# Scores of the first batch from float32 q and k, two heads on 64 rows each, in a fused attention and expert kernel

## The chip, the cores and the metric

The kernel runs on one core of one Trainium2 chip. The metric is the device time of one execution in microseconds (us). Three runs of the kernel before took 1341.06, 1344.57 and 1346.83 us; their median, 1344.57 us, is the time before.

## The reference: what is computed

Three layers in a row, in float32:

```python
# attention: batch 4, 8 heads, 576 tokens, head size 64; q, k, v are randn * 0.1
scores = scale * np.matmul(q, k.transpose(0, 1, 3, 2))
kth = np.partition(scores, -top_k, axis=-1)[..., -top_k:-top_k + 1]
mask = scores >= kth
scores = np.where(mask, scores, -1000000000.0)
...
return np.matmul(attn, v).astype(np.float32)
# gated layer: x is (2304, 512), w_gate and w_val (512, 1536), w_out (1536, 512)
gate = 1.0 / (1.0 + np.exp(-(x @ w_gate)))
val = x @ w_val
return (gate * val @ w_out).astype(np.float32)
# experts: 8 of (512, 1024) and (1024, 512), the two best of a token by noisy logits
h = np.maximum(x[mask] @ w1[e], 0.0)
out[mask] += top2_w[mask, k, None] * (h @ w2[e])
```

`top_k` is 32 and `scale` is 1/8. Which 32 scores of a row are kept, and which two experts a token goes to, are choices between close numbers, so products are carried to more than float16 throughout.

## The kernel before, in words

The work goes in order of the batch: for each of 4 batches, 5 tiles of queries (four of 128 rows, one of 64) and 4 pairs of heads make up the units, 20 a batch. A unit with 128 queries holds two tiles of scores, one for each head of the pair; a unit with the last 64 queries holds one tile, the two heads above each other. So a batch has 36 tiles of scores, each 128 by 576.

What happens to a tile: TensorE makes the scores into the one score buffer `ps` of two banks, 288 keys in each (line 348, or 351 for the tile of 64 queries); ScalarE copies them to `sS` (line 356); VectorE finds candidates, eight instructions a tile (line 365), and the best of them (lines 371 and 374); GpSimd scales two of these into a bias and a cut (line 391, with the constants `facs`); ScalarE takes the sign of score minus cut (line 400) and the exponential (line 383); GpSimd multiplies score and sign (line 406); VectorE ranks that (line 413) and masks the exponentials (line 428). Then TensorE transposes them (lines 457, 475, 477), ScalarE copies the transposes out, and TensorE multiplies with v in float32 (line 498), each head on 64 columns of the array. `xch` holds the result for a chunk of tokens, and once a chunk is full the gated layer runs on it (lines 538 and 577); the experts come at the end (lines 808 and 834).

Score products run in float16. Each number is split into two halves, a high one (the number times 64, rounded to float16) and a low one (what is left). For the first batch, `kq_ops` with `first` set loads k and q of a head pair twice each, so that all 64 dimensions of a head stand on rows 0 to 63 and again on rows 64 to 127 (line 216). ScalarE makes high halves (lines 220 and 221), VectorE the low ones (lines 222 and 224); q ends up with the high half above and the low half below, and k has high halves in both places in one tile and low halves in both in another. A product over 128 rows is then (q high + q low) times one half of k, and two of them, summed in the bank, make the score. Later batches get the same halves by another route (lines 235 to 252): ScalarE and GpSimd make them, and DMAs put them in place.

Weights of the gated layer come as pairs of 32-bit words and are unpacked in 36 pieces of 512 KB (`weight_piece`, line 275 on): VectorE takes the upper words apart (lines 281, 282), ScalarE the lower ones (283), GpSimd adds them (286), then halves are made (287, 289, 291, 292). Pieces are staged in the buffers `st`, three of them, which the q and k of the kernel before also use.

The order in which instructions stand on each engine is made before the program runs, by `Plan`: every operation is given with an engine, a planned duration, a priority, what it depends on and which buffers it takes and frees; `Plan.run` plays this through and issues, on each engine, the ready operation with the lowest priority number whose buffers are free. `CAPS` has the number of buffers of each kind: 3 `st`, 5 `khl`, 6 `sS`, 1 `ps`. Each engine then runs its instructions strictly in that order, and an instruction that waits holds all behind it. SP issues the loads, in order too.

## Time and profile before

| | |
|---|---|
| median of three runs | 1344.57 us |
| the profiled execution | 1342.8 us, its span 1341.0 us |
| TensorE busy (PE) | 1193.8 us, 89% |
| VectorE busy (DVE) | 872.2 us, 65% |
| ScalarE busy (ACT) | 800.6 us, 60% |
| GpSimd busy (POOL) | 743.0 us, 55% |
| score products of tiles with 128 queries (line 348), 512 records | 95.2 us |
| granted TensorE clock, mean | 0.955 |

Read it as a program of several parts, since the shares of the whole span mix them. The span begins with attention of the first batch and the unpacking of weights, goes on with attention and the gated layer beside each other, and ends with the experts. A granted clock of 1.00 stands for 2.4 GHz and 0.50 for 1.2 GHz; a value between is a mean over both.

### The profile page before, as it was taken

The numbers are of one execution on the slowest core, as the hardware profiler recorded it, in microseconds if no ns is written. First come the engines' busy times: TensorE is split into PE (matmuls) and PEld (weight loads), VectorE is DVE, ScalarE is ACT, GpSimd is POOL, SyncE is SP. The second block draws the span as 40 slices with busy tenths as digits, with TensorE's granted clock in tenths as the row PEclk, the third lists the DMA queues.
The fourth block names the chain that finished last, engine by engine and source line by source line (L and its number), as shares of the span: only waits on it lengthen the run. The fifth ranks groups of instructions, "written<-read, shape, count | busy, mean of one in ns | idle before, by whom it ended". The sixth has DMA issues, their size and how long they took to land. (4 is left out here: it accounts for less than half of the span.)

```text
span 1341.0 us, 29639 instructions
## 1 busy us (share of the span) xinstructions
PE 1193.8 (89%) x10669; PEld 878.2 (65%) x10670; DVE 872.2 (65%) x3616; ACT 800.6 (60%) x1796; POOL 743.0 (55%) x1004
## 2 busy tenths in 40 slices
PE   2456478699999999999999999989999999999997
PEld 1235356487676777786786876877666666676674
DVE  5998998888788688788888778545114234243111
ACT  4767778787777777786787776755214334243221
POOL 2789998788476776666775566342322222322221
PEclk9668689799899999999999999999999999999999
DMA  8433332344002500003300001357636576576441
GB/s 179 141 95 117 125 111 71 97 114 171 17 2 72 158 1 10 10 9 92 106 2 1 19 9 33 111 153 218 109 67 177 98 182 168 111 194 129 73 74 22
DMA packets 105616, 122.30 MB, mean 91 GB/s; under 512 B 56689, under 2 KB 66033, under 8 KB 105458
## 3 DMA queue, kind: packets, MB, share of 16 engines
q1 hardware_dynamic: 95346, 100.33, 27.5%
q0 software_dynamic: 10112, 19.97, 8.0%
q8 instruction: 86, 1.41, 0.4%
q14 instruction: 72, 0.59, 0.2%
HBM read 79.58 MB, written 20.63 MB: 75 GB/s over the span
## 5 line engine op out<-in xcount | busy, mean ns | idle before, releaser
L538 PEld LDWEIGHTS <-w 128*128 128x128 f16 x3456 | 275.3, 100 | 49.4 <-issue 21.7
L538 PE MATMUL mm<-xch,w 128*128 128x256 f16 (+1 forms) x2880 | 284.1, 254 | 17.8 <-DVE th L548 8.2
L816 DVE SCALAR_TENSOR_TENSOR g<-mm,g 128x256 f16<-128x256 f32 (+1 forms) x192 | 71.9, 379 | 242.5 <-ACT g L813 235.0
L406 POOL TENSOR_TENSOR y<-sS,sg 128x576 f32<-128x576 f32 x144 | 194.3, 1349 | 9.1
L808 PE MATMUL mm<-xch,w 128*128 128x256 f16 (+1 forms) x2016 | 190.3, 255 | 0.0
L808 PEld LDWEIGHTS <-w 128*128 128x128 f16 x2016 | 170.3, 98 | 23.4
L365 DVE MAX8 cand<-sS 128x8 f32<-128x72 f32 x1152 | 166.7, 217 | 21.6 <-ACT sS L356 21.2
L834 PEld LDWEIGHTS <-g 128*128 128x128 f16 x960 | 92.7, 98 | 105.6 <-DVE g L816 2.8
L577 PE MATMUL mm<-w,g 128*128 128x512 f16 x648 | 156.5, 385 | 4.1 <-POOL w L292 2.2
L428 DVE SCALAR_TENSOR_TENSOR e<-sS,good,e 128x576 f32<-128x576 f32 x144 | 144.7, 1026 | 2.1 <-ACT e L383 1.1
L348 PE MATMUL ps<-khl,qs 128*128 128x288 f16 x512 | 95.2, 315 | 57.0 <-ACT sS L356 39.4
L790 POOL DMA_INDIRECT v<-xd,ids x40 | 47.6, 1190 | 167.7 <-DVE ws L780 162.2
L813 ACT ACTIVATE g<-mm 128x256 f16<-128x256 f32 (+1 forms) x192 | 66.2, 347 | 118.0 <-PE mm L808 110.1
L846 POOL DMA_INDIRECT out<-e,ids x40 | 63.8, 1594 | 127.3 <-ACT e L843 58.7
L400 ACT ACTIVATE sg<-sS,m 128x576 bf16<-128x576 f32 x144 | 110.5, 769 | 35.4 <-POOL m L391 35.4
L413 DVE MAX8 good<-y 128x8 f32<-128x584 f32 x144 | 109.9, 763 | 28.6 <-POOL y L406 24.1
L555 POOL TENSOR_TENSOR g<-th,g 128x128 f16<-128x128 f32 (+1 forms) x144 | 92.5, 646 | 62.2 <-ACT g L552 59.6
L498 PE MATMUL tp<-pt,v 128*64 128x128 f32 (+3 forms) x1600 | 117.5, 285 | 5.4 <-ACT pt L464 2.6
L834 PE MATMUL tp<-w,g 128*128 128x512 f16 x504 | 115.3, 379 | 1.2 <-DVE g L816 1.2
L498 PEld LDWEIGHTS tp<-pt,v 128*64 128x64 f32 (+1 forms) x1600 | 85.0, 143 | 41.0 <-issue 23.9
L457 PE MATMUL tp<-ident,e 128*128 128x128 f32 x576 | 89.5, 292 | 24.6 <-DVE e L428 23.5
L577 PEld LDWEIGHTS <-g 128*128 128x128 f16 x648 | 63.0, 99 | 69.6 <-issue 8.5
(162 smaller groups left out, 2069.4 us busy)
## 6 DMA issues: line engine op xcount, KB each, us to landing
st<-w SPq DMA_DIRECT2D x64, 512.0 KB
khl<-st SPq DMA_DIRECT2D x48, 144.0 KB
st<-w_gate SPq DMA_DIRECT2D x12, 512.0 KB
st<-w_val SPq DMA_DIRECT2D x12, 512.0 KB
st<-w_out SPq DMA_DIRECT2D x12, 512.0 KB
st<-k_t SPq DMA_DIRECT2D x20, 288.0 KB
st<-q_t SPq DMA_DIRECT2D x20, 288.0 KB
out<-x SPq DMA_DIRECT2D x6, 768.0 KB
```

Source lines behind the costliest of these rows:

```text
L348: P.matmul(o, kqr.qs[:, t, u.q0:u.q0 + 128], kqr.khl[:, c, t, ks], start=c == 0, stop=c == 1)
L365: V.max(T[t].cand[:, 8 * c:8 * c + 8], T[t].s[:, 72 * c:72 * c + 72])
L400: A.activation(T[t].sg, T[t].s, AF.Sign, scale=-CUT[0], bias=T[t].m[:, 25:26], accum_out=T[t].m[:, 26:27])
L406: G.tensor_tensor(T[t].y[:, :S], T[t].s, T[t].sg, op=OP.mult)
L413: V.max(good[:, TILES - 1 - u.i - t:TILES + 7 - u.i - t], T[t].y)
L428: return lambda: V.scalar_tensor_tensor(T[t].e, T[t].s, good[:, TILES + 6 - u.i - t:TILES + 7 - u.i - t], T[t].e, op0=OP.is_ge, op1=OP.mul ...
L498: P.matmul(u.po[64 * s:64 * s + 64, :], VB[u.b, kb][1][:k, (2 * u.hp + s) * D:(2 * u.hp + s + 1) * D], rhs, start=kb == 0, stop=kb == NK - 1)
L538: P.matmul(r.ps[:, a, :], wt.t[:, a, c, kb, fo:fo + 128], ch.x[x][:, kb, :], start=i == 0, stop=i == 11)
L555: G.tensor_tensor(r.g[:, 1], r.th, r.g[:, 0], op=OP.subtract)
L577: P.matmul(r.ps, g[:, c, 128 * t:128 * t + 128], WO[f // 4].t[:, d, f % 4, :], start=f == 0 and i == 0, stop=f == 11 and i == 2)
L808: P.matmul(r.ps, W[kb].w[c][:, 0, f * 128:f * 128 + 128], q.x[:, 4 * x + kb, :], start=i == 0, stop=i == 11)
L834: P.matmul(r.ps, gs[f].g[:, c, 128 * t:128 * t + 128], W[4 + f // 2].w[d][:, f % 2, :], start=f == 0 and i == 0, stop=f == 7 and i == 2)
```

## The change

For the first batch, no halves are made. `kq_ops` loads k and q of a head pair once each, as float32, straight into the buffer that held the halves of k (two pictures of 576 float32 numbers fill a `khl` buffer exactly); head 0 of the pair then stands on rows 0 to 63, head 1 on rows 64 to 127. The score product of a head takes those 64 rows of q and of k, in float32, one product for each 288 keys. Since q and k are no longer scaled by 64 each, the factor in the exponential and in `facs` is 1/8 for the first batch, and `SC` has an entry for each batch. Batches 1 to 3 are as before. The planned duration of a tile's score product is 0.9 us in the first batch, 0.5 us in the others.

```diff
-SC = 1.0 / (8.0 * SQ * SQ)
+
+SC = [1.0 / 8.0] + [1.0 / (8.0 * SQ * SQ)] * (B - 1)
...
-    facs = const.tile([128, 2], FT, name="facs")
-    G.memset(facs[:, 0:1], -SC)
-    G.memset(facs[:, 1:2], CUT[1])
+    facs = const.tile([128, 2, 2], FT, name="facs")
+    G.memset(facs, CUT[1])
+    for b in range(2):
+        G.memset(facs[:, b, 0:1], -SC[b])
...
-                hs = [plan.tile("st") for _ in range(2)]
-                st = {}
-
-                def load(w, src):
-                    def f():
-                        if w == "k":
-                            tiles()
-                        st[w] = tile_of("st", [128, 2, S], FT)
-                        for h in range(2):
-                            nc.sync.dma_start(st[w][64 * h:64 * h + 64], src[b, hp].rearrange("(s d) n -> d s n", s=2))
-                    return f
-                lk = op("SP", 1.6, prio, load("k", kT), alloc=[hs[0], r.h], lat=3.0)
-                lq = op("SP", 1.6, prio, load("q", qT), [lk], alloc=[hs[1]], lat=3.0)
-                a = op("ACT", 1.06, prio, lambda: A.activation(r.khl[:, 0], st["k"], AF.Copy, scale=SQ), [lk], use=[hs[0], r.h])
-                c = op("ACT", 1.06, prio, lambda: A.activation(r.qs, st["q"], AF.Copy, scale=SQ), [lq, a], use=[hs[1], r.h])
-                d = op("DVE", 1.3, prio, lambda: V.scalar_tensor_tensor(
-                    r.khl[:, 1], st["k"], SQ, r.khl[:, 0], op0=OP.mult, op1=OP.subtract), [a], use=[hs[0], r.h])
-                e = op("DVE", 1.3, prio, lambda: V.scalar_tensor_tensor(
-                    r.qs[64:], st["q"][64:], SQ, r.qs[64:], op0=OP.mult, op1=OP.subtract), [c], use=[hs[1], r.h])
-                r.done = [d, e]
+                def load():
+                    t = work.tile([128, 2, 2, S], FH, name="khl", bufs=CAPS["khl"])
+                    work.tile([128, 2, S], FH, name="qs", bufs=CAPS["khl"])
+                    r.kq = t.rearrange("p a b s -> p (a b s)").bitcast(FT).rearrange("p (c s) -> p c s", c=2)
+                    nc.sync.dma_start(r.kq[:, 0], kT[b, hp])
+                    nc.sync.dma_start(r.kq[:, 1], qT[b, hp])
+                r.done = [op("SP", 1.6, prio, load, alloc=[r.h], lat=3.0)]
...
+                    if u.b == 0:
+                        for j in range(2):
+                            for s in (t,) if u.nt == 2 else range(2):
+                                d = slice(64 * s, 64 * s + 64)
+                                P.matmul(T[t].ps[:, j, :288] if u.nt == 2 else T[t].ps[d, j, :288], kqr.kq[d, 1, u.q0:u.q0 + n],
+                                         kqr.kq[d, 0, j * 288:j * 288 + 288], start=True, stop=True)
+                        return
...
-                a = op("PE", 0.5 if u.nt == 2 else 0.5, prio, qk, kqr.done, alloc=[hp_], use=[kqr.h])
+                a = op("PE", 0.5 if u.b else 0.9, prio, qk, kqr.done, alloc=[hp_], use=[kqr.h])
...
-                    A.activation(T[t].e, T[t].s, AF.Exp, bias=T[t].m[:, CM:CM + 1], scale=SC)
+                    A.activation(T[t].e, T[t].s, AF.Exp, bias=T[t].m[:, CM:CM + 1], scale=SC[u.b])
```

`Plan` makes another order of it. On SP, at the start of the program, the loads stood like this before (line 216 loads k and q, 260 v, 941 and 942 the router's noise):

```order
L216 DMA st<-k_t 64x2x576 x2
L216 DMA st<-q_t 64x2x576 x2
L260 DMA v<-v_s 128x512 x4
L260 DMA v<-v_s 64x512
L216 DMA st<-k_t 64x2x576 x2
L216 DMA st<-q_t 64x2x576 x2
L216 DMA st<-k_t 64x2x576 x2
L941 DMA nst<-noise 128x4x8
```

And on SP at the same place now (213 and 214 load k and q, 249 v, 264 a piece of weights, 937 noise; line numbers are of the changed kernel):

```order
L213 DMA khl<-k_t 128x576
L214 DMA khl<-q_t 128x576
L249 DMA v<-v_s 128x512 x4
L249 DMA v<-v_s 64x512
L213 DMA khl<-k_t 128x576
L214 DMA khl<-q_t 128x576
L264 DMA st<-w_gate 128x2x512 x2
L264 DMA st<-w_val 128x2x512
L213 DMA khl<-k_t 128x576
L214 DMA khl<-q_t 128x576
L264 DMA st<-w_val 128x2x512
L213 DMA khl<-k_t 128x576
```

The doubled loads are single ones, and four pieces of weights moved up between the head pairs, ahead of the noise.

On VectorE (DVE), its first instructions before; 222 and 224 are the low halves, 365 candidates, 371 and 374 the best of them, 413 ranks, 428 masks:

```order
L222 SCALAR_TENSOR_TENSOR khl<-st,khl 128x1152
L224 SCALAR_TENSOR_TENSOR qs<-st,qs 64x1152
L365 MAX cand<-sS 128x8 x8
L222 SCALAR_TENSOR_TENSOR khl<-st,khl 128x1152
L365 MAX cand<-sS 128x8 x8
L224 SCALAR_TENSOR_TENSOR qs<-st,qs 64x1152
L371 MAX m<-cand 128x8 x2
L374 MATCH_REPLACE cand<-m,cand 128x64 x2
L371 MAX m<-cand 128x8 x2
L374 MATCH_REPLACE cand<-m,cand 128x64 x2
L371 MAX m<-cand 128x8 x2
L222 SCALAR_TENSOR_TENSOR khl<-st,khl 128x1152
```

On VectorE now, from the last best-of instructions of the first unit on (367; 361 is candidates, 270 and 271 the unpacking of a piece of weights, 409 ranks, 424 masks):

```order
L367 MAX m<-cand 128x8 x2
L270 TENSOR_SCALAR x_197<-st 128x512
L271 SCALAR_TENSOR_TENSOR x_197<-st,x_197 128x512
L361 MAX cand<-sS 128x8 x8
L270 TENSOR_SCALAR y<-st 128x512
L271 SCALAR_TENSOR_TENSOR y<-st,y 128x512
L270 TENSOR_SCALAR x_244<-st 128x512
L271 SCALAR_TENSOR_TENSOR x_244<-st,x_244 128x512
L409 MAX good<-y 128x8 x2
L424 SCALAR_TENSOR_TENSOR e,m<-sS,good,e 128x576 x2
L361 MAX cand<-sS 128x8 x8
```

The halves are gone, and three pieces of weights are unpacked between the first unit's best-of and its ranks; before, the first piece came after the fifth tile's candidates.

On TensorE (PE), the end of the fourth tile's scores and what follows before (348 scores, 457, 475 and 477 transposes):

```order
L348 LDWEIGHTS qs
L348 MATMUL ps<-khl,qs 128x288
L457 MATMUL tp<-ident,e 128x128 x8
L348 LDWEIGHTS qs
L348 MATMUL ps<-khl,qs 128x288
L348 LDWEIGHTS qs
L348 MATMUL ps<-khl,qs 128x288
L348 LDWEIGHTS qs
L348 MATMUL ps<-khl,qs 128x288
L348 LDWEIGHTS qs
L348 MATMUL ps<-khl,qs 128x288
L475 MATMUL tp<-ident,px 128x128
```

And TensorE's first instructions now (336 scores, two rows a tile; 453, 471 and 473 transposes, 494 the product with v); a float32 product has its weight load in it and is one row here:

```order
L336 MATMUL ps<-khl 128x288 x10
L453 MATMUL tp<-ident,e 128x128 x8
L336 MATMUL ps<-khl 128x288 x2
L471 MATMUL tp<-ident,px 128x128
L473 MATMUL tp<-ident,e 64x128 x2
L494 MATMUL tp<-pt,v 64x128 x10
L336 MATMUL ps<-khl 128x288 x4
```

Before, four tiles' scores stood ahead of the first transposes; now five do, the fifth of them from the third pair of heads.

## Rows read from the trace of the kernel before

**Rows 1.** The page: busy us (share of the span) and instructions of each engine.
```profile
PE 1193.8 (89%) x10669; PEld 878.2 (65%) x10670; DVE 872.2 (65%) x3616; ACT 800.6 (60%) x1796; POOL 743.0 (55%) x1004
```

**Rows 2.** Windows: from:to, length, busy us of PE, PEld, DVE, ACT, POOL, clock.
```profile
0.00:40.00 40.00, 11.67 (x55) 7.01 (x57) 23.38 (x87) 21.00 (x33) 10.95 (x37) 1.00 0.76 176
40.00:80.00 40.00, 15.24 (x70) 9.23 (x70) 39.03 (x122) 30.06 (x58) 33.61 (x36) 0.57 0.40 121
80.00:120.00 40.00, 28.64 (x301) 23.91 (x301) 38.08 (x134) 29.05 (x67) 36.08 (x42) 0.79 0.33 105
120.00:160.00 40.00, 19.03 (x153) 13.42 (x150) 37.07 (x112) 29.35 (x65) 37.90 (x41) 0.72 0.39 124
160.00:200.00 40.00, 28.34 (x264) 20.07 (x264) 39.10 (x129) 30.11 (x69) 39.07 (x40) 0.81 0.37 118
200.00:240.00 40.00, 34.99 (x372) 26.31 (x371) 34.87 (x147) 31.17 (x72) 33.49 (x44) 0.96 0.22 60
240.00:280.00 40.00, 29.20 (x274) 20.99 (x272) 34.16 (x187) 31.13 (x73) 31.56 (x48) 0.83 0.40 101
280.00:320.00 40.00, 39.32 (x371) 32.35 (x368) 34.69 (x158) 33.79 (x80) 36.90 (x54) 1.00 0.70 219
```

**Rows 3.** Timeline of VectorE: start us, length us, instructions, idle before and its releaser.
```profile
13.54 1.18 DVE L365 MAX8 cand<-sS 128x8 f32<-128x72 f32 x8 [1.92 <-ACT sS L356]
...
29.68 0.80 DVE L428 SCALAR_TENSOR_TENSOR e<-sS,good,e 128x576 f32<-128x576 f32 x1
```

**Rows 4.** VectorE from 0 to 40 us by line: busy us, mean ns, idle before.
```profile
L224 DVE SCALAR_TENSOR_TENSOR qs<-st,qs 64x1152 f16<-64x1152 f32 x4 | 5.4, 1355 | 0.6 <-ACT qs L221 0.4
L222 DVE SCALAR_TENSOR_TENSOR khl<-st,khl 128x1152 f16<-128x1152 f32 x4 | 5.4, 1354 | 10.2 <-ACT khl L220 10.1
```

**Rows 5.** Timeline of ScalarE, first 21 us.
```profile
6.03 1.28 ACT L220 ACT_TABLE_LOAD   x1 [5.90 <-DMA st<-k_t]
...
12.85 0.65 ACT L356 ACTIVATE sS<-ps 128x576 f32<-128x576 f32 x1 [2.62 <-PE ps L348]
15.21 1.16 ACT L220 ACTIVATE khl<-st 128x1152 f16<-128x1152 f32 x1 [1.71 <-DMA st<-k_t]
...
20.91 1.16 ACT L220 ACTIVATE khl<-st 128x1152 f16<-128x1152 f32 x1 [1.95 <-DMA st<-k_t]
```

**Rows 6.** Timeline of TensorE: scores and the product with v, early and late.
```profile
35.44 1.11 PE L348 MATMUL ps<-khl,qs 128*128 128x288 f16 x4 [0.98 <-ACT sS L356]
36.48 2.38 PE L498 MATMUL tp<-pt,v 128*64 128x128 f32 x20
...
500.03 0.65 PE L348 MATMUL ps<-khl,qs 128*128 128x288 f16 x4 [0.37 <-ACT sS L356]
...
528.99 1.09 PE L498 MATMUL tp<-pt,v 128*64 128x128 f32 x16
```

**Rows 7.** TensorE records, ns min/median/max: v before 100, in 320:600 us, a float32 weight load.
```profile
L498 PE MATMUL tp<-pt,v x80: 269/421/476, 36.5 to 92.3; 128*64 128x128 f32 x64, 64*64 64x128 f32 x16
L498 PE MATMUL tp<-pt,v x580: 218/273/476, 321.2 to 598.5; 128*64 128x128 f32 x134, 64*64 64x128 f32 x33, 128*64 128x64 f32 x21, 64*64 64x64 f32 x6
L623 PEld LDWEIGHTS tp<-wr,y x144: 186/190/333, 220.1 to 920.6; 128*128 128x128 f32 x144
```

**Rows 8.** DMA issues from 0 to 60 us: count and KB each.
```profile
st<-k_t SPq DMA_DIRECT2D x8, 288.0 KB
...
st<-w_gate SPq DMA_DIRECT2D x4, 512.0 KB
```

**Rows 9.** Timeline of GpSimd: the router's weights.
```profile
24.21 0.24 POOL L947 TENSOR_SCALAR wr<-wr 128x64 f32<-128x64 f32 x1 [20.75 <-DMA wr<-wn]
```

**Rows 10.** Windows of TensorE's score products alone: line 348 twice, then line 351.
```profile
80.00:200.00 120.00, 13.00 (x56) 6.60 (x55) 0.77 0.36 115
200.00:250.00 50.00, 3.27 (x20) 1.79 (x20) 0.97 0.26 67
...
200.00:250.00 50.00, 2.72 (x32) 1.71 (x32) 0.97 0.26 67
```

More of the change, by code (lines that the diff above doesn't have):

```diff
@@ L377, in top @@
                         V.tensor_copy(good[:, TILES + 6 - u.i - t:TILES + 7 - u.i - t], T[t].m[:, 31:32])
-                    V.tensor_scalar(u.m[:, :, 32], u.m[:, :, 0], -SC, None, op0=OP.mult)
+                    V.tensor_scalar(u.m[:, :, 32], u.m[:, :, 0], -SC[u.b], None, op0=OP.mult)
             def ex(t):
@@ L391, in attention @@
                 c2 = op("POOL", 0.15, prio - 1, lambda: G.tensor_tensor(
-                    u.m[:, :, 24:26], u.m[:, :, 0:24:23], facs[:, None, :].to_broadcast([128, u.nt, 2]), op=OP.mult),
+                    u.m[:, :, 24:26], u.m[:, :, 0:24:23], facs[:, min(u.b, 1), None, :].to_broadcast([128, u.nt, 2]), op=OP.mult),
                     [c2], use=[u.hm])
```

## The prediction, made before the result was known

> **What bounds the kernel now.** I read the page's busy table first [rows 1], then the busy time of each engine in stretches of 40 us [rows 2], then single engines in order of time in the first 40 us [rows 3 to 5], and last the TensorE rows that price a float32 product [rows 6, 7]. The page calls TensorE the busy engine: 1193.8 us of a span of 1341.0, which leaves 147 us in which it does nothing [rows 1]. The stretches say where those lie: from 0 to 200 us TensorE is busy for 103 of 200 us, from 200 to 280 us for 64 of 80, from 280 on for all but 1 us in 40 [rows 2]. So there are two parts. Late, TensorE sets the pace and its work is fixed. Early it waits, and what it waits for is VectorE and GpSimd: from 40 to 200 us VectorE is busy 37 to 39 of each 40 us and GpSimd 34 to 39 [rows 2]. The end moves by as much as the state that the kernel has reached at about 280 us comes sooner or later. The first 40 us are a third thing: there VectorE is busy for 23.4 us only and GpSimd for 11 [rows 2]. Its first real work, the candidates of the first scores, starts at 13.54 us [rows 3], although the first k had landed at 6.0 us [rows 5]; between lie halves of k and of q.
>
> **What goes.** Eight VectorE instructions, four of 1.354 and four of 1.355 us [rows 4], are 10.8 us. All have run by 38 us, so they stand in the stretch before VectorE is full, but each of them ahead of candidates, ranks or weights on the same in-order engine. Eight ScalarE instructions of 1.16 us [rows 5] are 9.3 us; ScalarE is busy 21 of the first 40 us and about 30 of 40 later [rows 2], so I price them at nothing by themselves. And half of the loads of q and k: before, 8 of k [rows 8] and as many of q, 288 KB each, after, half of them, so 2.36 MB fewer. The pace of the queue is seen between the second k, landed at 15.21, and the third, landed at 20.91 [rows 5]: two double loads, 1.18 MB, in 5.7 us, or 207 KB per us. 2.36 MB are 11.4 us of that queue.
>
> **What moves.** The first product now waits, on TensorE itself, for one load of k and one of q, as many bytes as the two loads of k that had landed at 6.0 us. The table load of ScalarE, 1.28 us, stood behind that landing [rows 5] and has nothing to wait for in the changed order. So: product from 6.0 us, 2.15 us long (below), copy 0.65 us [rows 5], first candidates at 8.8 us in place of 13.54. Staging buffers are no longer taken by q and k, so three weight pieces are loaded ahead of the third head pair's k, and their unpacking on VectorE comes right after the first candidates. That fills VectorE earlier, and GpSimd with it. The new wait has a queue behind it: TensorE's fifth score tile, the third head pair's first, stands ahead of the first unit's transposes, and its k and q are the last of 4.5 MB, which at 207 KB per us land at 22 us. The first unit's masks come at about that time (before, from 29.7 us on [rows 3]), so I price this wait at nothing; each us by which the loads are later delays the first unit by as much, and the gaps below hold that. One memset more or less among GpSimd's constants and a scale that is 1/8 in place of a smaller number cost nothing: GpSimd idles for 20.75 us right after them [rows 9].
>
> Dead time of VectorE in the first 40 us before: 40.0 less 23.4 idle is 16.6, and 10.8 of halves, together 27.4 us [rows 2, 4]. After: 8.8 us until the first candidates; then the second tile's product waits for the first copy, since there is one score buffer, 2.15 + 0.65 less 1.18 for the candidates of a tile [rows 3], 1.6 us; then weights. The fifth piece stands behind 8 loads of q and k, 1152 KB of v and four pieces of 512 KB [rows 8], 5.6 MB, which is 27 us at that pace, and behind the small loads of noise and router weights, the last of which kept GpSimd waiting until 24.2 us before [rows 9] and lies later now. I put 5 us of idle there: an estimate, between nothing and 11. Sum 15.4 us, so the lead of VectorE is 27.4 less 15.4, 12 us. GpSimd had 29 us idle in the same stretch [rows 2] and its work follows VectorE's, so it can keep that lead. The ends: no gap at all behind the first candidates gives 27.4 less 8.8, 18.6 us; everything held by the queue and by GpSimd as before, and only the earlier start left, gives 13.54 less 8.8, 4.7 us.
>
> **What comes.** No float32 product of 288 columns is in the trace; the nearest is that of the probabilities with v. It shows two records for each product, and two products side by side on 64 columns each, so that 20 records are ten steps of 128 columns. They took 2.38 us at 36.48; 16 records, eight steps, took 1.09 us at 528.99 [rows 6]. Taking off the length of the last record (0.421 and 0.273 [rows 7]) leaves nine steps of 0.218 us in the early part, at the low level of TensorE's clock, and seven of 0.117 later, at the high one. Half of 0.218 is 0.109, and I take that. For 288 columns it is 0.49 and 0.245 us a step. A tile needs four such steps now (two halves of the keys, two records each), 1.96 or 0.98 us and a tail of 0.19 or 0.17. Before it took four float16 records: 1.11 us and 0.65 us in all [rows 6]. So a tile's scores cost TensorE 1.0 us more at 1.2 GHz, 0.5 us more at 2.4 GHz, and 36 tiles 18 to 36 us. Bounds: at best the 64-row product runs in the time of the float16 one, nothing added; at worst the weight load, 0.190 us for a float32 one of 128 columns [rows 7], is not hidden behind the step before, another 0.76 us a tile.
>
> Where it falls decides. In 200 to 250 us there were 20 records of four a tile and 32 of eight a tile [rows 10], 9 tiles, at a granted clock of 0.97: 9 times 0.49 is 4.4 us. The other 27 ran before 200 us, where TensorE has 97 us idle [rows 2] while VectorE is full: that covers them. TensorE is busy 80% there [rows 2], so I charge 80%, 3.5 us; the bounds are 0 and 4.4 plus 9 times 0.76, 11.2 us. If the cover in the early part is gone, the other 27 tiles cost 27 times 0.5 to 1.0, 13 to 27 us; that is a rival below.
>
> Here a rule of the Trainium skill speaks against the change. In the rows, a product on 64 columns that follows one on 128 starts 0.07 us before that one's end (36.48 against 35.44 + 1.11 [rows 6]), while records of one block overlap by some 0.2 us (0.421 long, 0.218 apart), so a switch shows as a delay near 0.13 us at most. TensorEngine Tiling (Array Packing), section Key Properties, says that changing the tiling mode, not just the tile, drains the engine, and scores on 64 rows are such a change. By it two switches for each of the 9 late tiles add 2.3 us, and the sum would be 1336.6 in place of 1334.3; the 54 switches of the early tiles lie in idle time. The trace neither shows nor excludes it for rows.
>
> **Sum.** Lead 12 less 3.5, a gain of 8.5 us. The profiled execution took 1342.8 us (span 1341.0): 1334.3, and I say 1334. That is 10.6 us under the median of the three runs shown, 1344.57, of which 1.8 is the profiled run's own distance.
>
> **The rivals.** First, the front gains and loses it again: 1342. The 12 us exist in VectorE alone; GpSimd, at 38 to 39 of 40 us in 120 to 200 us [rows 2], decides when scores are ranked and weights are ready, and small loads that now lie behind four weight pieces hold it, since its router-weight scaling stands in order ahead of the second unit's work. Lead 4.7 less 3.5, about 1. For it: GpSimd is as full as VectorE later. Against it: GpSimd was idle for 29 of the first 40 us, so it too can start sooner.
>
> Second, nothing is lost: VectorE finds work all the way from 8.8 us, weights arrive in time and TensorE hides every added step: 18.6 us, 1324. For it: the weight unpacking is there to fill gaps. Against it: the 5.6 MB ahead of the fifth piece.
>
> Third, slower: TensorE becomes the chain before 200 us. Place: the tiles from 80 us on, 14 before 200 (56 records [rows 10]) and the 9 late ones, where gated-expert products stand in the same in-order queue and TensorE was already busy 28 of 40 us in two of three stretches at a clock of 0.72 to 0.81 [rows 2]. If the others then wait for it there, the steps of those tiles come onto the chain at 0.5 to 1.0 us each, with the late ones 11 to 18 us, against the lead of 4.7 to 12. It decides from the point at which added steps there exceed the lead: 1342.8 plus 15 less 5, 1353. Against it: 44 us idle in that part [rows 2].
>
> **How the numbers follow.** Forecast 0.55, lead lost 0.22, nothing lost 0.12, slower 0.11. A measurement of this kernel can tell about 0.5%, 6.7 us, from no change; with the median 1344.57 the bounds are 1337.8 and 1351.3. Of the forecast, whose own range is 1328 to 1340, I count four fifths as faster: 0.44, with 0.12 of the second rival and 0.02 of the first 0.58. Slower: two thirds of the third rival and a little for an order of work that happens to fit worse, 0.10. The rest, 0.32, is no change. The range goes from the best bound (18.6 and no erosion, 1324) to the worst of the likely ones (lead 4.7, late cost 9, 1347); above it lies most of the third rival.
>
> **What would show it.** Right: first candidates on VectorE at 8.5 to 9.5 us, the ranks of the first unit near 20 us in place of 27; VectorE busy over 30 of the first 40 us; score products of the first batch in records spaced near 0.49 us early and 0.245 us warm; TensorE busier by 18 to 36 us in total and the stretch in which it is first full reached 6 to 12 us sooner. Wrong: VectorE idle for long stretches between 10 and 40 us (the queue), TensorE waited for by the score copies in 100 to 200 us (third rival), or score steps far from these lengths.

## The result, and the profile after

| | before | after |
|---|---|---|
| median of the runs compared | 1342.82 us (1340.51 to 1346.83, 4 runs) | 1324.73 us (1323.60 to 1325.92, 4 runs) |
| profiled execution, span | 1342.8, 1341.0 us | 1323.6, 1321.9 us |

The ratio is 0.9868, with an interval of 0.9854 to 0.9883: 18.1 us faster. The sign was forecast, and the time lies at the lower end of the range; the forecast itself, 1334, is more than 9 us off, and the gain is over twice the 8.5 us of the sum.

The page of the changed kernel, busy us (share of the span) and instructions of each engine:

```profile
PE 1228.2 (93%) x10669; PEld 896.4 (68%) x10670; DVE 869.1 (66%) x3608; ACT 791.6 (60%) x1788; POOL 740.9 (56%) x1005
```

TensorE does 34.4 us more than in [rows 1], in a span that is 19.1 us shorter: its idle time fell from 147 to 94 us. Where, the windows of the changed kernel show (columns as in [rows 2]):

```profile
0.00:40.00 40.00, 24.06 (x71) 13.57 (x72) 26.61 (x98) 23.71 (x46) 25.50 (x50) 0.95 0.65 198
40.00:80.00 40.00, 23.20 (x86) 13.78 (x85) 39.52 (x133) 29.85 (x58) 36.71 (x38) 0.54 0.43 127
80.00:120.00 40.00, 32.88 (x262) 24.84 (x263) 39.12 (x124) 29.36 (x66) 36.16 (x39) 0.65 0.37 110
120.00:160.00 40.00, 30.12 (x278) 21.59 (x273) 31.08 (x81) 26.73 (x64) 36.12 (x43) 0.86 0.38 123
160.00:200.00 40.00, 36.67 (x311) 25.06 (x311) 35.73 (x154) 30.78 (x67) 33.79 (x42) 0.89 0.34 101
200.00:240.00 40.00, 31.84 (x259) 22.02 (x258) 37.78 (x167) 31.06 (x70) 30.79 (x42) 0.88 0.22 52
240.00:280.00 40.00, 34.40 (x340) 26.93 (x338) 38.79 (x190) 31.56 (x76) 32.46 (x51) 0.95 0.32 83
280.00:320.00 40.00, 39.34 (x339) 29.42 (x337) 37.69 (x184) 32.68 (x76) 35.14 (x50) 1.00 0.50 171
```

Against [rows 2], VectorE is busy 26.6 us of the first 40 in place of 23.4, though 10.8 us of halves [rows 4] are gone from it, and GpSimd 25.5 in place of 11. From 40 to 280 us both are about as full as before, and TensorE stands idle for 46 us less up to 280 us.

VectorE of the changed kernel in order of time (start us, length us, instructions, idle before and its releaser; line 361 is candidates, 270 unpacking, 409 ranks, 424 masks):

```profile
7.47 1.18 DVE L361 MAX8 cand<-sS 128x8 f32<-128x72 f32 x8 [7.35 <-ACT sS L352]
10.50 1.18 DVE L361 MAX8 cand<-sS 128x8 f32<-128x72 f32 x8 [1.85 <-ACT sS L352]
...
13.15 0.41 DVE L270 TENSOR_SCALAR x<-st 128x512 int32<-128x512 int32 x1
...
18.78 0.77 DVE L409 MAX8 good<-y 128x8 f32<-128x584 f32 x1
...
20.72 1.01 DVE L424 SCALAR_TENSOR_TENSOR e<-sS,good,e 128x576 f32<-128x576 f32 x1
```

The first candidates start 6.1 us sooner than in [rows 3], the first masks 9 us sooner, and a piece of weights is unpacked from 13.2 us on. In the trace the 36th piece is through VectorE's first step at 176 us (before 205). The last ranks of the first batch, its 36th tile's, end at 263.3 us (before 277.5); first of the kernel before, then of the changed one:

```profile
276.72 0.76 DVE L413 MAX8 good<-y 128x8 f32<-128x584 f32 x1
```

```profile
262.52 0.77 DVE L409 MAX8 good<-y 128x8 f32<-128x584 f32 x1
```

TensorE of the changed kernel, the same columns; line 336 is the new score product, 534 and 573 are the gated layer:

```profile
4.50 2.25 PE L336 MATMUL ps<-khl 64*128 64x288 f32 x4 [4.50 <-DMA khl<-q_t]
7.49 2.29 PE L336 MATMUL ps<-khl 64*128 64x288 f32 x4 [0.74 <-ACT sS L352]
...
27.53 2.28 PE L336 MATMUL ps<-khl 64*128 64x288 f32 x4 [2.86 <-ACT sS L352]
...
33.54 1.23 PE L336 MATMUL ps<-khl 64*128 64x288 f32 x4 [0.58 <-ACT sS L352]
...
41.47 2.29 PE L336 MATMUL ps<-khl 64*128 64x288 f32 x4 [1.23 <-ACT sS L352]
...
212.36 1.51 PE L534 MATMUL mm<-xch,w 128*128 128x128 f16 x24
213.80 1.23 PE L336 MATMUL ps<-khl 64*128 64x288 f32 x4
214.97 1.25 PE L573 MATMUL mm<-w,g 128*128 128x512 f16 x5
```

A tile of scores takes 2.25 to 2.29 us early and 1.23 us late, where it took 1.11 and 0.65 before [rows 6]. The window around the tile at 41.47 us has a granted clock of 0.50, the level of 1.2 GHz:

```profile
40.00:44.00 4.00, 2.53 (x6) 1.16 (x4) 4.00 (x24) 2.73 (x6) 3.23 (x4) 0.50 0.41 129
```

For the first 36 us the profile shows a granted clock of 1.00, and there tiles took 2.25 to 2.29 us at first and 1.23 us at 33.54. So for the rows of the first 36 us, the level is read from the lengths alone; the granted clock doesn't show it.

**How the span is split from here on.** At 280 us a kernel has some of TensorE's work left. What the span loses or gains is then two numbers: the work left at 280 us, and the time in which TensorE stands idle after it. Both come from two windows, here of the kernel before and then of the changed one:

```profile
0.00:280.00 280.00, 167.12 (x1482) 120.95 (x1483) 245.70 (x911) 201.88 (x429) 222.67 (x282) 0.81 0.41 115
280.00:1400.00 1120.00, 1026.70 (x9191) 757.23 (x9187) 626.50 (x2706) 598.74 (x1368) 520.35 (x723) 0.99 0.33 80
```

```profile
0.00:280.00 280.00, 213.17 (x1594) 147.79 (x1595) 248.63 (x939) 203.06 (x444) 231.51 (x301) 0.82 0.39 113
280.00:1400.00 1120.00, 1014.99 (x9079) 748.57 (x9077) 620.49 (x2670) 588.49 (x1345) 509.38 (x704) 0.99 0.33 79
```

Before: 1026.7 us of work left, and 1341.0 - 280 - 1026.7 = 34.3 us idle. After: 1015.0 left, 11.7 less, and 26.9 idle, 7.4 less. The sum is the 19.1 us between the spans. So part of the gain was made before 280 us, where the forecast looked for it, and part behind, where the forecast had nothing. These splits come from one execution each, and two profiles of one and the same kernel below differ by 7.5 us in work left and by 0.8 us in idle time; where a timed ratio and a split disagree, the ratio counts.

### The profile page after: what moved, and what is told of

Read it like the earlier page. It is cut to its first block, busy times and chain, and to the rows that moved or that the text cites. A ratio compares the mean times of both kernels' runs of the same rounds, so it can differ in the third digit from the quotient of the medians.

```text
span 1321.9 us, 29643 instructions
## 1 busy us (share of the span) xinstructions
PE 1228.2 (93%) x10669; PEld 896.4 (68%) x10670; DVE 869.1 (66%) x3608; ACT 791.6 (60%) x1788; POOL 740.9 (56%) x1005
## 5 line engine op out<-in xcount | busy, mean ns | idle before, releaser
L424 DVE SCALAR_TENSOR_TENSOR e<-sS,good,e 128x576 f32<-128x576 f32 x144 | 155.5, 1099 | 2.3 <-ACT e L379 1.5
L453 PE MATMUL tp<-ident,e 128*128 128x128 f32 x576 | 91.6, 296 | 17.2 <-DVE e L424 15.7
L379 ACT ACTIVATE e<-sS,m 128x576 f32<-128x576 f32 x144 | 106.5, 768 | 0.2
```

The source lines that it names most:

```text
L379: A.activation(T[t].e, T[t].s, AF.Exp, bias=T[t].m[:, CM:CM + 1], scale=SC[u.b])
L424: return lambda: V.scalar_tensor_tensor(T[t].e, T[t].s, good[:, TILES + 6 - u.i - t:TILES + 7 - u.i - t], T[t].e, op0=OP.is_ge, op1=OP.mul ...
```

## The experiments

The theory to begin with was the forecast's, with larger terms: VectorE starts sooner and loses no time to halves. The rival was that the order which the plan made moves the kernel by itself. In the expectations these are theories A and B. Theory C, from the first results on, is that the early part is worth some 12 us by itself and the rest is an accident of the later order; theory D is that all of the gain is the change's own. All ratios are to the kernel before, run beside it on the same chip, with 95% intervals; 0.5% is 6.7 us. A difference of two ratios, such as "slower than the changed kernel", carries both their intervals, some 3 to 4 us either way.

**The order of before kept.** Loads and scores as in the change, but the plan is given the old operations, of which those for halves issue nothing. Each engine has the order of the kernel before without the halves.

```diff
...
+                no = lambda: None
+                lk = op("SP", 1.6, prio, load(0), alloc=[hs[0], r.h], lat=3.0)
+                lq = op("SP", 1.6, prio, load(1), [lk], alloc=[hs[1]], lat=3.0)
+                a = op("ACT", 1.06, prio, no, [lk], use=[hs[0], r.h])
+                c = op("ACT", 1.06, prio, no, [lq, a], use=[hs[1], r.h])
+                d = op("DVE", 1.3, prio, no, [a], use=[hs[0], r.h])
+                e = op("DVE", 1.3, prio, no, [c], use=[hs[1], r.h])
+                r.done = [d, e]
...
-                a = op("PE", 0.5 if u.b else 0.9, prio, qk, kqr.done, alloc=[hp_], use=[kqr.h])
+                a = op("PE", 0.5, prio, qk, kqr.done, alloc=[hp_], use=[kqr.h])
```

> The change's loads and float32 scores, with every engine's other instructions in the order of the kernel before: the plan is told of the halves and issues nothing for them. Theory A (the removed VectorE work, the shorter start and the loads are the gain): most of it stays, 1328 to 1332 us. Theory B (the gain is the new order, in which weights are loaded and unpacked 26 to 30 us earlier): little stays, 1337 to 1343.

Measured: 0.9960 (0.9943 to 0.9978), 5.4 us faster, between what the two theories gave. A third of the gain is there without any new order. The window of its first 40 us shows why it is less:

```profile
0.00:40.00 40.00, 26.26 (x73) 15.28 (x75) 20.70 (x100) 18.07 (x36) 15.19 (x45) 1.00 0.47 144
```

Its first candidates start at 7.41 us, as early as in the changed kernel; but VectorE does 20.7 us of work by 40 us, against 26.6 in the changed kernel and 23.4 less 10.8, 12.6, of the same work in the kernel before. So the halves and the wait for them are worth a lead of 8.1 us in VectorE, and the weight pieces that the plan moved up another 5.9.

The same kernel once more:

> The changed loads and scores in the order of the kernel before, once more: 0.996 at first, 3 to 8 us, where its one profile showed 12.7 us. If the change is worth 12 us by itself in an unchanged order: 0.990 to 0.992. If 5 us: 0.995 to 0.997.

Measured: 0.9957 (0.9943 to 0.9972), the same. Its split is 4.4 us less work left and 1.6 us less idle; the first profile of this kernel had 11.9 and 0.8. That is how far a split can be trusted.

**Eight instructions given back to VectorE, not waited for.** They write what nobody reads; the plan holds them at 0 us, so nothing else moves.

```diff
...
+                for _ in range(2):
+                    op("DVE", 0.0, prio, lambda: V.scalar_tensor_tensor(
+                        r.x, r.kq, SQ, r.kq, op0=OP.mult, op1=OP.subtract), [a], use=[r.h])
```

> The changed kernel with eight VectorE instructions of the size of the removed ones put back, for which nothing waits; the order of all else is unchanged. Their results are not used. Two of the eight fall into the time before the first scores. Theory A: the other six, 8.2 us, are paid in full or in large part, 1330 to 1334 us. Theory B: under 3 us, 1325 to 1328.

Measured: 0.9937 (0.9916 to 0.9958), 9.3 us slower than the changed kernel. The eight took 1.498 us each in the mean (line, engine, operation, names, shapes, count | busy us, mean ns | idle before), and two of them ran while VectorE would have waited for its first scores:

```profile
L218 DVE SCALAR_TENSOR_TENSOR qs<-khl 128x1152 f16<-128x1152 f32 x8 | 12.0, 1498 | 4.5 <-DMA khl<-q_t 4.4
```

```profile
4.49 2.75 DVE L218 SCALAR_TENSOR_TENSOR qs<-khl 128x1152 f16<-128x1152 f32 x2 [4.37 <-DMA khl<-q_t]
7.49 1.18 DVE L365 MAX8 cand<-sS 128x8 f32<-128x72 f32 x8 [0.26 <-ACT sS L356]
```

The candidates start at 7.49 us, as in the changed kernel (7.47), so those two put nothing off. The other six are 12.0 less 2.75, 9.2 us of VectorE, and the end moved by 9.3 us: within the intervals, all of it.

**Eight that the scores wait for.** As above, but in place on q and k, with the scores behind them (a number times 1, and the larger of it and itself, so q and k stay what they are). The order of all else is the same, but for one tile of scores that moved behind four transposes and a first instruction of ScalarE.

```diff
...
+                for _ in range(2):
+                    a = op("DVE", 0.0, prio, lambda: V.scalar_tensor_tensor(
+                        r.kq, r.kq, 1.0, r.kq, op0=OP.mult, op1=OP.max), [a], use=[r.h], lat=0.0)
+                r.done = [a]
```

> The changed kernel with eight VectorE instructions put back that the scores of their head pair wait for (each writes k and q over with the same numbers), order unchanged: the removed work and the wait for it, with the new loads and the new order. Front lead by the prediction's sum: 12 less 10.8 of work less 2.7 of start, near 0; with theory C the later 7 us stay, 1333 to 1337. If the front's lead comes from the order, weights first, and not from the removed halves: 1327 to 1331.

Measured: 0.9945 (0.9925 to 0.9964), 10.3 us slower than the changed kernel, and the first candidates at 10.44 us in place of 7.47. Here all eight, 12.0 us, put VectorE's other work off. The two experiments differ by 1 us, less than their intervals, so whether the 3 us by which the first scores come later are paid as well is not shown.

**More work for TensorE.** The first half of the keys is multiplied twice.

```diff
-                        for j in range(2):
+                        for j in (0, 0, 1):
```

> The changed kernel with the first of the two products of each score tile of the first batch issued twice, in unchanged order: some 28 to 31 us more of TensorE work, about as much as the change itself added. If TensorE's added work is hidden (theory A and B): 1325 to 1331 us. If TensorE is the chain there (the third rival): 1340 to 1355.

Measured: 0.9950 (0.9932 to 0.9968), 11 us slower than the changed kernel for 20.5 us more of TensorE's time (1248.7 against 1228.2): less work than expected, and a time between the two that were expected. So the cover of early TensorE work is not free. In part it delays VectorE: the first candidates start at 8.48 us, and VectorE is busy for 24.5 us of the first 40, where the changed kernel has 7.47 and 26.6. By the split 4.1 us of it come before 280 us and 4.6 after; with the scatter of splits that division is open.

**More bytes in the queue.** k is loaded a second time into a part that is not used, 1.18 MB.

```diff
...
+                    nc.sync.dma_start(x.rearrange("p a s -> p (a s)").bitcast(FT), kT[b, hp])
```

> The changed kernel with each k of the first batch loaded a second time into the unused second part of its buffer: 1.18 MB more on the queue in the first 20 us, order of all engines unchanged. If the queue sets the pace of the first 40 us (the prediction counted 11 us for 2.36 MB): 3 to 6 us slower, 1327 to 1330. If VectorE and GpSimd do: within 2 us of the changed kernel.

Measured: 0.9876 (0.9852 to 0.9899), the changed kernel's time within the interval. By the pace of 207 KB per us these bytes would have been 5.7 us of queue. VectorE waited once for a piece of weights, 0.78 us, and the end does not show it: the queue sets no pace here.

**The changed kernel again:**

> The changed kernel once more, on the chip and in the rounds of the runs beside it, as their measure. By the first result 0.987 of the kernel before; 1322 to 1326 us where that takes 1340 to 1343.

Measured: 0.9865 (0.9847 to 0.9883). The result repeats. So does its split: 14.6 us less work left and 6.3 less idle; the kernel with doubled loads, in the same order, has 16.2 and 4.5. With the first profile, the mean of three is 14.2 before 280 us and 6.1 behind.

**Another planned duration for the first batch.** The number changes no instruction, only the order. 0.5 in place of 0.9:

```diff
-                a = op("PE", 0.5 if u.b else 0.9, prio, qk, kqr.done, alloc=[hp_], use=[kqr.h])
+                a = op("PE", 0.5 if u.b else 0.5, prio, qk, kqr.done, alloc=[hp_], use=[kqr.h])
```

> The changed kernel with 0.5 in place of 0.9 as the planned duration of a score product of the first batch: the same instructions, in another order on every engine. It shows how much of the time hangs on the accident of the order. Theory A: within 4 us of the changed kernel, 1321 to 1329. If order alone can move the end by more: anything from 1315 to 1340.

Measured: 0.9913 (0.9887 to 0.9938), 6 us slower than the changed kernel. And 2.0:

```diff
+                a = op("PE", 0.5 if u.b else 2.0, prio, qk, kqr.done, alloc=[hp_], use=[kqr.h])
```

> The changed kernel with 2.0 in place of 0.9 as planned duration of a score product of the first batch, near what it takes at 1.2 GHz: another order from the start. Front within 3 us of the changed kernel's; by the scatter of the later order so far (-3 to +7 us) the end anywhere from 1318 to 1332.

Measured: 0.9989 (0.9974 to 1.0004): nothing is left of the gain, by an order alone, and it is slower than was expected. Here the loss lies before 280 us, and not behind it:

```profile
280.00:1400.00 1120.00, 1025.57 (x9175) 757.12 (x9174) 628.09 (x2701) 596.23 (x1362) 515.21 (x717) 0.99 0.32 79
```

That is 1025.6 us of work left, almost as much as in the kernel before, and 1334.9 - 280 - 1025.6 = 29.3 us idle. So an order can lose the front as well, although 2.0 is nearer to what an early tile takes.

**Another planned duration for the later batches**, in the changed kernel and in the kernel before, so that each change is compared under several orders. In the changed kernel 0.7, 0.4 and 0.6 in place of 0.5:

```diff
-                a = op("PE", 0.5 if u.b else 0.9, prio, qk, kqr.done, alloc=[hp_], use=[kqr.h])
+                a = op("PE", 0.7 if u.b else 0.9, prio, qk, kqr.done, alloc=[hp_], use=[kqr.h])
```

> The changed kernel with the same planned 0.7 for batches 1 to 3, order as in the changed kernel until the end of the first batch. Theory C: the lead at 280 us stays at 11 to 13 us (as TensorE idle saved less TensorE work added), the end moves by up to 7 us, 1324 to 1331. Theory D: lead and end both stay, 1322 to 1326.

> The changed kernel with 0.4 in place of 0.5 as planned duration of the score products of batches 1 to 3: front as in the changed kernel, 11 to 15 us, and a third sample of the later order: 1318 to 1332.

> The changed kernel with 0.6 there. Theory C: 1320 to 1340 us, most likely 1328 to 1334, the mean of the changed orders so far. Theory D (the gain of 18 us is the change's own): 1322 to 1326.

And in the kernel before:

```diff
-                a = op("PE", 0.5 if u.nt == 2 else 0.5, prio, qk, kqr.done, alloc=[hp_], use=[kqr.h])
+                a = op("PE", 0.7 if u.b else 0.5, prio, qk, kqr.done, alloc=[hp_], use=[kqr.h])
```

> The kernel before with 0.7 in place of 0.5 as planned duration of the score products of batches 1 to 3: the same instructions, another order from about the second batch on. Theory C (the front is worth 12 us by itself, the other 7 us of the gain are an accident of the later order): the kernel before can be moved by order alone, to anything between 1333 and 1345 us. Theory D (all of the gain follows from the earlier front): it stays within 2 us, 1338 to 1342.

> The kernel before with 0.4 in place of 0.5 as planned duration of the score products of batches 1 to 3, the partner of the changed kernel with the same number, which gained nothing (1.000). Theory C (an order has its own accident, some us either way, and the change has a worth of 6 to 14 us beside it): 1330 to 1350 us, each way as likely. Theory E (the number 0.4 is bad for both): 1346 to 1356.

> The kernel before with 0.6 there. Theory C: 1330 to 1350 us. If the kernel before is near the middle of its orders: 1338 to 1346.

Measured:

| planned for later batches | kernel before | changed kernel | change, us |
|---|---|---|---|
| 0.4 | 1.0067 (1.0043 to 1.0091) | 1.0000 (0.9989 to 1.0012) | -9.0 |
| 0.5 (as they are) | 1 | 0.9868 (0.9854 to 0.9883) | -17.7 |
| 0.6 | 0.9995 (0.9980 to 1.0010) | 0.9934 (0.9913 to 0.9956) | -8.2 |
| 0.7 | 1.0019 (1.0007 to 1.0032) | 0.9929 (0.9913 to 0.9945) | -12.1 |

(The last column is the difference of the ratios times 1342.8 us.) Under each number the change gains, 8 to 18 us with a mean of 11.7. The order alone moves the kernel before by 9.7 us between its best and its worst, the changed one by 17.7. The pair that was measured as the result is the one with the largest gain. The changed kernel with 0.4 and with 0.7 is slower than was expected.

What an order does can be seen where it does it. The changed kernel with 0.4, its first 280 us and what follows:

```profile
0.00:280.00 280.00, 213.42 (x1606) 148.09 (x1608) 246.88 (x917) 201.45 (x443) 230.51 (x300) 0.82 0.38 112
280.00:1400.00 1120.00, 1018.47 (x9065) 746.90 (x9063) 620.64 (x2691) 589.43 (x1347) 512.92 (x706) 0.99 0.32 79
```

And with 0.7:

```profile
0.00:280.00 280.00, 212.75 (x1597) 146.18 (x1599) 248.55 (x941) 202.42 (x443) 231.62 (x301) 0.82 0.38 113
280.00:1400.00 1120.00, 1013.16 (x9074) 746.28 (x9072) 618.81 (x2669) 589.78 (x1346) 508.18 (x704) 0.99 0.33 79
```

On every engine the order of both is that of the changed kernel up to 254 us at least. Both have reached 280 us with the same TensorE work done as the changed kernel (213.4 and 212.8 against 213.2 us), and the last ranks of the first batch at the same time (263.6 us in both, against 263.3). Their spans are 1339.0 and 1330.7 against 1321.9. TensorE's idle time behind 280 us is 1339.0 - 280 - 1018.5 = 40.5 us in the one, 37.5 in the other, and 26.9 in the changed kernel (28.0 in its second profile). One place where it arises, the kernel with 0.4:

```profile
340.00:360.00 20.00, 11.54 (x72) 7.91 (x73) 19.30 (x103) 14.84 (x31) 11.57 (x17) 0.67 0.01 1
360.00:380.00 20.00, 17.94 (x154) 14.46 (x150) 16.55 (x87) 12.61 (x31) 12.77 (x21) 0.90 0.01 1
```

and the changed kernel in the same stretch:

```profile
340.00:360.00 20.00, 18.14 (x177) 15.75 (x176) 15.66 (x78) 15.84 (x33) 12.19 (x18) 1.00 0.08 27
360.00:380.00 20.00, 19.74 (x187) 16.78 (x185) 18.24 (x105) 14.29 (x38) 12.27 (x19) 1.00 0.01 1
```

With 0.4, TensorE idles 8.5 us of the 20, and its clock is granted at 0.67 in them. TensorE's waits from 335 to 380 us there (engine, line, what it waited for: us, times, longest):

```profile
PE tp L471 <- POOL xch L507: 3.1, 1, 3.1
PE ps L344 <- ACT sS L352: 1.9, 2, 1.0
PE tp L453 <- DVE e L424: 1.7, 1, 1.7
```

Transposes stand at TensorE's head and wait for other engines' work on batches behind the first, whose last ranks were over at 263.6 us. These instructions are the same in both kernels; only their order differs.

**One pair of heads alone.** Float32 for the first pair of the first batch, halves for the other three.

```diff
+F32 = (0,)
...
+            u.w = 0 if u.b == 0 and u.hp in F32 else 1
...
-                    if u.b == 0:
+                    if not u.w:
```

> Only the first head pair's scores from float32 q and k, single loads for it; the other three pairs with halves, double loads and staging as in the kernel before. Six of the eight VectorE instructions stay. If the front comes from each pair's halves in proportion, and from the earlier start: front 6 to 8 us; if nearly all of it is the removed wait of the first scores: 10 to 12 us. The later order, new again, adds -3 to +7: 1329 to 1338 us.

Measured: 1.0080 (1.0056 to 1.0104), slower than before, a miss of the theory.

```profile
0.00:40.00 40.00, 16.85 (x63) 9.13 (x64) 25.32 (x109) 22.63 (x38) 16.08 (x42) 0.95 0.73 181
```

Its first candidates come early too, at 7.83 us. Of VectorE's 25.3 us, six half-making instructions are some 8, which leaves 17.2, a lead of 4.6 us over the kernel before. Yet it has 1034.6 us of work left at 280 us, 7.9 more than the kernel before. It has an order of its own as well, and what of it is that order was not separated.

## Why the prediction was right and wrong

**The step that failed** is the sentence on which the sum stands: "Late, TensorE sets the pace and its work is fixed. The end moves by as much as the state that the kernel has reached at about 280 us comes sooner or later." The work is fixed, but not the idle time: it was 34.3 us before, and over the kernels run it went from 26.9 to 43.4. The prediction saw that there is some ("from 280 on for all but 1 us in 40", read from one stretch) and then treated it as constant. Yet [rows 1] less the first 280 us of [rows 2] is 1026.7 us of work in 1061: the 34.3 us idle are four times the gain that was forecast. The two changed kernels above, with the same TensorE work done at 280 us and spans 9 and 17 us longer, show that the plan's order from about 255 us on moves the end. In the result it happened to fit better, by 7.4 us in the first profile and 6.1 in the mean of three. The forecast had an order that fits better or worse as "a little" of its slower case, and no term for it in the sum.

**The terms before 280 us.** The sum was 12 less 3.5, 8.5 us; the three profiles of this order have 11.7, 14.6 and 16.2. The lead was a little undersized: VectorE's dead time is 40.0 - 26.6 = 13.4 us against 15.4, a lead of 14.0. The sign "VectorE busy over 30 of the first 40 us" did not come, and it does not follow from the sum either: 40 less 15.4 is 24.6. The first product started at 4.50, not 6.0 us, since one load of k and one of q came sooner than two of k had, and the first candidates at 7.47, ahead of the window of 8.5 to 9.5. The gap of 1.6 us behind them was 1.85. The ranks of the first unit came at 18.8 us, as said ("near 20"). The idle behind that, 13.4 less 7.5 less 1.85, was 4.1 against the 5 that were laid to weights coming late. That it came near was luck, since no load ended any of these waits; GpSimd ended 2.6 us of them and ScalarE 1.3; the longest of each:

```profile
29.71 0.69 DVE L278 SCALAR_TENSOR_TENSOR w<-x,w 128x512 f16<-128x512 f32 x1 [1.03 <-ACT w L276]
...
32.64 0.77 DVE L409 MAX8 good<-y 128x8 f32<-128x584 f32 x1 [1.17 <-POOL y L402]
```

**The cost of the float32 scores.** The length of a tile was right where it was taken from the rows: 2.25 to 2.29 us against 2.15 early, and 1.23 against 0.98 and a tail of 0.17 late. Within a tile the records start 0.48 us apart early and 0.24 late, as said, but for the first two (0.61 and 0.35 us). That the early rows ran at the lower level of the clock, as the prediction has it, is read from their lengths: the granted clock of that stretch is 1.00 [rows 2]. What a tile takes of TensorE's time was too low. Around 213.80 us the changed kernel's tile is 1.23 us long, starts 0.07 us before the block ahead of it ends, and ends 0.06 us after the next one starts. In the kernel before the same place reads

```profile
213.23 0.83 PE L538 MATMUL mm<-xch,w 128*128 128x128 f16 x12
213.90 0.65 PE L348 MATMUL ps<-khl,qs 128*128 128x288 f16 x4
214.39 0.83 PE L538 MATMUL mm<-xch,w 128*128 128x128 f16 x12
```

and the tile is 0.65 us long, with 0.16 us of overlap at each end. So a warm tile costs 0.58 us more by its length and 0.19 us more by its two ends, together 0.77, not 0.49. (The ends of TensorE's records are modelled. By starts alone, from the tile's to that of the next block, it is 1.17 us against 0.49; that leaves out the end ahead of the tile.) Two things differ at such an end, the number type and the rows or columns of the array. These rows tell them apart, two of the changed kernel and then four of the kernel before:

```profile
222.21 1.23 PE L336 MATMUL ps<-khl 64*128 64x288 f32 x4 [0.47 <-ACT sS L352]
223.38 0.33 PE L471 MATMUL tp<-ident,px 128*128 128x128 f32 x1
```

```profile
222.43 0.29 PE L623 MATMUL tp<-wr,y 128*128 128x16 f32 x2
222.57 0.65 PE L348 MATMUL ps<-khl,qs 128*128 128x288 f16 x4
...
231.46 0.68 PE L351 MATMUL ps<-khl,qs 128*64 128x288 f16 x8
232.07 0.84 PE L538 MATMUL mm<-xch,w 128*128 128x128 f16 x12
```

From a float32 score tile on 64 rows to a float32 transpose on 128 the overlap is 0.06 us; from float32 to float16, both on 128 rows and 128 columns, it is 0.15; from float16 on 64 columns to float16 on 128 it is 0.07. So it is the change of the part of the array, and not of the type, that costs the 0.09 us, where 0.13 was set as its most. The Trainium skill, TensorEngine Tiling (Array Packing), Key Properties, says that a change of the tiling mode, not just of the tile, drains the engine; these rows agree. The forecast's sum put nothing for it, and its weighing of the rule put two new switches on each of the 9 late tiles. But the 4 of them with 64 queries stood on 64 columns before, and had such ends already (231.46 us above); they grew from 0.68 to 1.19 us (at 225.43 us of the changed kernel), by 0.51. If the others are like the two read here, the 9 late tiles cost 5 times 0.77 and 4 times 0.51, 5.9 us, where the forecast had 4.4; the switches are 1 us of that. In total TensorE had 34.4 us more to do, at the upper end of 18 to 36. Yet none of it can be seen as a loss before 280 us: a lead of 14.0 and a gain of 14.2 in the mean leave nothing for the 3.5. Doubling a part of this work on purpose did cost 11 us for 20.5, so that it is free is not shown; it may be paid by something else that the split doesn't tell apart.

**The queue.** 11.4 us of loads fewer were told of as part of the change, and the weights' idle of 5 us was laid to the pace of 207 KB per us. From 2 to 13 us the queue moved 352 KB per us in the changed kernel (the last number of a row) and 253 in the kernel before, first the changed one:

```profile
2.00:13.00 11.00, 6.83 (x12) 3.50 (x12) 3.68 (x29) 1.66 (x5) 1.23 (x15) 1.00 1.00 352
```

```profile
2.00:13.00 11.00, 1.14 (x4) 0.58 (x5) 2.71 (x2) 3.85 (x5) 1.20 (x14) 1.00 1.00 253
```

So the pace was set too low for the new loads. And 1.18 MB more cost nothing that can be measured, so the queue was no bound.

**What was right.** The halves are priced by two kinds of experiment: 9.2 and 12.0 us of VectorE's time, put back in its way, cost 9.3 and 10.3 us at the end; and taken out under the old order, with everything else kept, the halves and the earlier start bring 5.4 to 5.8 us after all costs. So time of VectorE in the early part is paid for at the end, as the forecast had it. ScalarE's table load waited for no landing; it starts at 0.83 us.

**The rivals.** The first, a lead lost again in GpSimd, fell: it was busy 25.5 us of the first 40, and its router-weight scaling started right behind the instruction ahead of it, with no wait for its load:

```profile
29.38 0.25 POOL L943 TENSOR_SCALAR wr<-wr 128x64 f32<-128x64 f32 x1
```

The second, nothing lost, has the right time by the wrong way: VectorE did stand idle for 6 us behind its first candidates, and what made up for it lies behind 280 us. The third, TensorE as the chain before 200 us, fell: from 80 to 200 us TensorE was idle for 20 us, half of before, and in that stretch ScalarE and VectorE waited for it for 4.4 us, where it was 8.5 before. But more work of this kind is not free, as the doubled products show.

**What stays open.** How the 18.1 us divide between the change and its order has two answers: 5.6 us with the old order kept, which gives the change no use of the buffers that come free, and 11.7 us as a mean over four pairs of orders, which is a mean over accidents. The forecast's 8.5 lies between. Why the kernel with one float32 pair is slower than both is not known. And each experiment that puts work into the changed kernel takes it out of an order that happens to fit: some of the 9 to 11 us that they cost may be that.

## What to carry to other kernels

Where a list scheduler sets the order, an edit is two edits: what it removes, and a new order for all that follows. Price the second by moving a planned duration that changes no instruction, in the kernel before and in the changed one; here that alone was worth 10 to 18 us, as much as the whole result, and it belongs in the range from the start. A stage that is "full" at 97% still has idle time, here 27 to 43 us over the kernels run, so the state at the end of the early stage does not fix the end.

## What was not expected of the hardware

A float32 score product on 64 rows between float16 products on 128 rows costs TensorE some 0.09 us at each end beside its own length, by the overlap of neighbouring records (0.07 and 0.06 in place of 0.16 us). A change of type alone, float32 to float16 on the whole array, keeps the overlap (0.15 us at 222.57 us of the kernel before). A change of rows alone, float32 to float32, does not (0.06 us at 223.38 us of the changed kernel), nor does one of columns alone (0.07 us at 232.07 us of the kernel before).
